# Constants in bf16, max-subtract matmuls behind other matmuls, and PSUM banks joined to the pool after the exponentials

## The chip, the cores and the metric

The kernel runs on one core of one Trainium2 chip. The metric is device microseconds of one execution; lower is better. A profile is one execution of its own: its span is about 2 us shorter than the time that the clock of the runs gives to the same execution (264.7 against 266.84 us for the profiled run of the kernel before).

## The reference

A block of two branches over one sequence of 2048 tokens of width 512, both fed by the same layernorm. Cut to what matters:

```python
xn = layernorm(x)
# branch A: 32 heads of 16, each token attends to 8 earlier tokens at distance 0, 2, ..., 14
q, k, v = split(xn @ wqkv)
logits  = sum_d q[s, d] * k[s - 2w, d] * scale          # w = 0..7, masked before the start
attn    = softmax(logits over w)
A       = (sum_w attn * v[s - 2w]) @ wo
# branch B: gated MLP with a mixing over tokens
z       = gelu(xn @ w_in);  z1, z2 = z[:, :896], z[:, 896:]
g       = w_sp @ layernorm(z2) + b_sp                    # w_sp is 2048 x 2048
B       = (z1 * g) @ w_out
out     = x + A + B
```

## The kernel before

The kernel is written as a list of operations with dependencies, estimated durations and priorities. A list scheduler runs once, when the kernel is built, and fixes the order of the instructions on each engine; the chip only sees that order and the semaphores. An operation's `margin` is added to the time at which the scheduler believes it to be ready. It is no wait on the chip: it makes the scheduler put other ready work of the same engine in front. PSUM is the buffer that matmuls write to, used here as eight banks of 128x512 f32; an eviction is the copy of a result out of its bank, after which the bank can be written again.

```python
# scheduler: when is an operation believed to be ready?
ready_t[u.seq] = max(d.done for d in u.deps) + self.HOP + u.margin

# constants: identity, head-sum matrix E and its transpose, loaded as f32 and cast on VectorE
_ldx(0, 1)
ld_cst = sc.dma(... e.dma_start(cfs, cdram.ap()) ...)        # 128 x 768 f32
_ldx(1, 1); _ldx(2, 1); _ldx(3, 1)                           # x tiles, then wq, wk, more x, wv, w_in
cv_id = sc.op("dve", ... tensor_copy(out=identb, in_=cf[:, 0:128]) ...)
# ... two more casts

banks = _Banks([0, 1, 2, 3])         # four PSUM banks rotate through T, QKV, Z2, Z1, G, output
# TensorE program: transposes of xn (T), then QKV (KQ), then V, Z2 (i = 0..15), Z1, G, output
# ... cut ...
# logits of row block u (512 tokens): VectorE multiplies q by the 8 shifted k (d1), TensorE sums
# over the 16 channels of a head with E (p1), four column groups t; u even uses banks 4,5, odd 6,7
d1 = sc.op("dve", ... tensor_tensor(out=pr, in0=qv, in1=kv, op=mult) ..., name="d1_%d_%d")
p1 = sc.op("pe", _p1, ..., prio=1, margin=pe_margin)         # pe_margin = 2500 ns
# after the fourth t: maximum over w, subtract it by a matmul, exponential, normalise
d2 = sc.op("dve", ... tensor_reduce(out=nm, in_=Lv, op=max, negate=True) ..., name="d2_%d")
p2 = sc.op("pe", _p2, [d2, cv_id], ..., name="p2_%d" % u, prio=1)      # no margin
ex = sc.op("act", ... activation(out=ep[:, u, :], in_=Lv, func=Exp, scale=0.25) ...)
# ... d3: sum, reciprocal, normalise on VectorE; later d4: probabilities times V on VectorE
```

In the text, "transpose" is T, "logit matmuls" are p1, "maximum" is d2 and "max-subtract matmuls" are p2. T, QKV, V, Z2 and Z1 are TensorE work with an eviction on ScalarE behind each group of four matmuls.

## Time and profile before

| | before |
|---|---|
| median of 15 runs | 267.33 us (266.36 to 268.94) |
| span of the profile | 264.7 us |
| TensorE (PE) busy | 94% |
| G stage starts in the chain of waits at | 127.04 us |
| last max-subtract matmuls at | 83.23 us |

The page's busy times and its 40 slices (each digit is the busy share of 6.6 us in tenths; PEclk is the clock that the record says was granted):

```profile
PE 247.8 (94%) x1655; PEld 118.5 (45%) x1682; DVE 196.8 (74%) x263; ACT 100.7 (38%) x166; POOL 55.5 (21%) x116
PE   6498996999996999999999999999999999999995
DVE  4798969999998999999322259799999997322332
PEclk9599999899999999999999999999999999999999
```

TensorE is full from the fourteenth slice on. VectorE (DVE) is full up to about the nineteenth, near 125 us. So there are two nearly full engines in the first 84 us; after that VectorE is still busy, but TensorE no longer waits for it.

The chain of waits of the kernel before, followed back from the last instruction (start, duration, what):

```profile
82.08 1.10 DVE negmax L665
...
83.23 0.60 PE ps L673 x2
83.83 19.04 PE ps L463 x100
...
127.04 8.20 PE ps L794 x38
```

Up to about 53 us the chain runs through QKV on TensorE and evictions on ScalarE, from there to 83 us mostly through VectorE; the last maximum (L665) releases the last max-subtract (L673), and from there on TensorE (L463 is Z2, L559 Z1, L794 G) follows itself without a gap. Whatever is won must be won before 84 us, and the kernel ends after the last max-subtract plus all the TensorE work that was not done before it.

The TensorE timeline of the kernel before (start, duration, engine, line, operation, tiles, count; in brackets the idle time in front and what ended it). L531 is QKV; 8 matmuls of 512 columns take 1.73 us start to start at full clock, 0.43 us each at half:

```profile
12.00 2.89 PE L531 MATMUL ps<-gh,rc 128*128 128x512 bf16 x7 [1.16 <-ACT gh L447]
14.95 1.89 PE L531 MATMUL ps<-gh,rc 128*128 128x512 bf16 x8
...
45.37 1.89 PE L531 MATMUL ps<-gh,rc 128*128 128x512 bf16 x4 [1.77 <-ACT gh L447]
47.48 2.22 PE L531 MATMUL ps<-gh,rc 128*128 128x512 bf16 x7 [0.22 <-issue]
...
79.54 1.69 PE L463 MATMUL ps<-gh 128*128 128x448 bf16 x8
83.23 0.60 PE L673 MATMUL ps<-negmax,identb 128*128 128x512 bf16 x2 [2.00 <-DVE negmax L665]
```

(The record of the first QKV matmul is missing here, as "x7" shows; the first weight load of the group is at 11.59 us. The 0.22 us in front of 47.48 us is such a missing record too, and no idle time.) Three losses stand out: a half-speed start, 1.77 us of waiting for a transpose eviction followed by about 3 us at half speed, and 2.00 us of waiting for the last maximum.

Why the 1.77 us: on ScalarE (ACT) that eviction (L447) stands behind the table load and the exponential of the first row block:

```profile
42.51 1.28 ACT L678 ACT_TABLE_LOAD   x1
43.80 1.02 ACT L678 ACTIVATE ep<-ps 128x1024 bf16<-128x1024 f32 x1
44.72 0.59 ACT L447 ACTIVATE gh<-ps 128x512 bf16<-128x512 bf16 x1
```

VectorE idles little in this stage. These are the largest idle times between 42 and 83 us, and the last maximum:

```profile
44.86 0.69 DVE L682 TENSOR_TENSOR gh<-ep 128x512 f32<-128x512 bf16 x1 [0.51 <-ACT ep L678]
53.57 1.22 DVE L665 TENSOR_REDUCE negmax<-ps 128x128 bf16<-128x1024 f32 x1 [0.71 <-PE ps L636]
81.45 0.51 DVE L490 TENSOR_SCALAR rb<-rb,mv,rs 128x896 bf16<-128x896 bf16 x1 [0.99 <-POOL rs L487]
82.00 1.17 DVE L665 TENSOR_REDUCE negmax<-ps 128x128 bf16<-128x1024 f32 x1
```

### The profile page before, as it was taken

To read this page: it belongs to the slowest core of one execution; us is meant where nothing else is said; L and a number is where in the kernel's file an instruction comes from. 1 tells how busy PE (TensorE), PEld (TensorE's weight loads), DVE (VectorE), ACT (ScalarE), POOL (GpSimd) and SP (SyncE) were. 2 spreads that over 40 slices of the span, in tenths; PEclk is the share of its full clock that TensorE was granted. 3 is DMA by queue.
4 is the path that set the end of the run, shared out by engine and by line. 5 is a ranking of instruction groups with operands and counts; after the bars stand their busy time and mean duration, and the time that the engine had idled before them with its cause. 6 is when DMAs were issued, how large, how long until landed. Compare 5 with 4: busy or idle time off the path is not lost.

```text
span 264.7 us, 4074 instructions
## 1 busy us (share of the span) xinstructions
PE 247.8 (94%) x1655; PEld 118.5 (45%) x1682; DVE 196.8 (74%) x263; ACT 100.7 (38%) x166; POOL 55.5 (21%) x116
## 2 busy tenths in 40 slices
PE   6498996999996999999999999999999999999995
PEld 5244453454453454444444444444444444444442
DVE  4798969999998999999322259799999997322332
ACT  3279876465577877677611111111011100000000
POOL 3568000201134544440000100000010030122200
PEclk9599999899999999999999999999999999999999
DMA  6999991030319920035699799788988860233331
GB/s 189 354 376 215 249 207 25 0 40 6 25 64 227 181 68 0 2 88 110 159 229 251 178 242 253 161 209 187 217 193 187 203 170 6 79 110 109 103 97 59
DMA packets 45969, 38.57 MB, mean 146 GB/s; under 512 B 34816, under 2 KB 42880, under 8 KB 43904
## 3 DMA queue, kind: packets, MB, share of 16 engines
q0 software_dynamic: 4160, 19.97, 34.0%
q1 hardware_dynamic: 41792, 18.35, 28.0%
q8 instruction: 13, 0.21, 0.4%
q14 instruction: 4, 0.03, 0.1%
HBM read 26.74 MB, written 3.15 MB: 113 GB/s over the span
## 4 chain that ended last, share of the span: by engine, by line
PE 77%; DVE 10%; ACT 6%; POOL 2%; issue 2%; DMA 1%; SPq 0%
PE ps L794 36%; PE ps L835 9%; PE ps L559 9%; PE ps L531 8%; PE ps L463 7%; DVE prod L629 6%; PE ps L846 5%; ACT kT L543 2%; ACT rc L512 2%; ACT gh L447 2%; DMA rc<-in_A_x_dram 1%; PE ps L636 1%; POOL pd_scratch L721 1%; ACT qT L543 1%; DVE negmax L665 1%
## 5 line engine op out<-in xcount | busy, mean ns | idle before, releaser
L531 PE MATMUL ps<-gh,rc 128*128 128x512 bf16 x180 | 46.1, 396 | 5.5 <-ACT gh L447 4.3
L794 PE MATMUL ps<-sa,rb 128*128 128x512 bf16 x220 | 48.3, 379 | 0.2
L794 PE MATMUL ps<-gh,rb 128*128 128x512 bf16 x219 | 48.2, 379 | 0.3
L787 ACT ACTIVATE ps<-xr 128x512 f32<-128x512 bf16 x28 | 16.8, 602 | 71.2 <-DVE rc L805 71.0
L629 DVE TENSOR_TENSOR prod<-qT,kT 128x4096 bf16<-128x4096 bf16 x16 | 36.2, 2276 | 2.5 <-ACT qT L543 1.4
L805 DVE TENSOR_TENSOR rc<-ps,rc 128x512 bf16<-128x512 f32 x28 | 19.2, 687 | 25.3 <-PE ps L794 25.3
L757 DVE TENSOR_TENSOR prod<-qT,vT 128x4096 bf16<-128x4096 bf16 x16 | 36.5, 2280 | 0.0
L794 PEld LDWEIGHTS ps<-gh,rb 128*128 128x128 bf16 x224 | 21.9, 98 | 26.4
L794 PEld LDWEIGHTS ps<-sa,rb 128*128 128x128 bf16 x224 | 21.9, 98 | 26.4
L856 DVE TENSOR_TENSOR stg<-ps,xr 128x512 bf16<-128x512 f32 x16 | 11.1, 692 | 26.9 <-PE ps L846 26.9
L729 POOL DMA_DIRECT2D qT<-pd_scratch x16 | 8.5, 530 | 104.1 <-DVE prod L757 44.4
L531 PEld LDWEIGHTS ps<-gh,rc 128*128 128x128 bf16 x192 | 18.1, 101 | 25.6 <-issue 4.8
L835 PE MATMUL ps<-sa,rc 128*128 128x512 bf16 x111 | 26.7, 379 | 0.1
L463 PE MATMUL ps<-gh 128*128 128x448 bf16 x128 | 25.0, 353 | 0.0
L559 PE MATMUL ps<-gh 128*128 128x512 bf16 x109 | 24.0, 379 | 0.2
L761 DVE TENSOR_TENSOR prod<-prod 128x2048 bf16<-128x2048 bf16 x16 | 19.5, 1219 | 0.1
L565 ACT ACTIVATE rc<-ps 128x512 bf16<-128x512 f32 x28 | 16.7, 595 | 6.7 <-PE ps L559 6.7
L470 ACT ACTIVATE rb<-ps 128x448 bf16<-128x448 f32 x32 | 16.8, 545 | 5.7 <-PE ps L463 5.6
L463 PEld LDWEIGHTS ps<-gh 128*128 128x128 bf16 x128 | 12.3, 98 | 11.8 <-ACT rb L470 0.4
L835 PEld LDWEIGHTS ps<-sa,rc 128*128 128x128 bf16 x112 | 11.0, 98 | 13.2
L559 PEld LDWEIGHTS ps<-gh 128*128 128x128 bf16 x112 | 11.0, 98 | 13.1
L846 PE MATMUL ps<-sa,kT 128*128 128x512 bf16 x62 | 16.2, 379 | 0.1
(55 smaller groups left out, 235.5 us busy)
## 6 DMA issues: line engine op xcount, KB each, us to landing
qT<-pd_scratch POOLq DMA_DIRECT2D x16, 1024.0 KB, 7.3
xr<-in_A_x_dram POOLq DMA_DIRECT2D x16, 128.0 KB, 2.4
out_dram<-stg SPq DMA_DIRECT2D x16, 128.0 KB, 1.7
gh<-in_B_w_in_dram SPq DMA_DIRECT2D x2, 896.0 KB, 10.1
rc<-in_A_wqkv_dram SPq DMA_DIRECT2D x2, 512.0 KB, 5.8
rc<-in_A_x_dram SPq DMA_DIRECT2D x2, 512.0 KB, 7.9
pd_scratch<-ep POOLq DMA_DIRECT2D x4, 256.0 KB, 10.1
sa<-in_B_w_out_dram SPq DMA_DIRECT2D x1, 896.0 KB, 9.1
```

Source lines behind the costliest of these rows:

```text
L463: ins = e.matmul(ps[:, bk, 0:448], xnT[:, k, 128 * i:128 * i + 128], w_in[:, k, 896 + 448 * hf:896 + 448 * hf + 448], start=(k == 0), stop ...
L470: ge = sc.op("act", lambda e, i=i, hf=hf, bk=bk: e.activation(out=z2[:, i, 448 * hf:448 * hf + 448], in_=ps[:, bk, 0:448], func=ACTF.Gelu_ ...
L531: ins = e.matmul(ps[:, bk, :], wP[:, k, which * 512 + 128 * t:which * 512 + 128 * t + 128], xnT[:, k, 512 * n:512 * n + 512], start=(k == ...
L559: ins = e.matmul(ps[:, bk, :], w_in[:, k, 128 * m:128 * m + 128], xnT[:, k, 512 * n:512 * n + 512], start=(k == 0), stop=(k == 3))
L629: d1 = sc.op("dve", lambda e, pr=pr, qv=qv, kv=kv: e.tensor_tensor(out=pr, in0=qv, in1=kv, op=ALU.mult), deps, dur=t_dve(4096, 2), name="d ...
L757: d4a = sc.op("dve", lambda e, b=b, vv=vv: e.tensor_tensor(out=tmp8.rearrange("p (w s) -> p w s", w=8), in0=pbS[b].rearrange("p (w s) -> p ...
L761: d4b = sc.op("dve", lambda e: e.tensor_tensor(out=tmpA, in0=tmp8[:, 0:2048], in1=tmp8[:, 2048:4096], op=ALU.add), [d4a, d4c_prev], dur=t_ ...
L787: pre = sc.op("act", lambda e, n=n, bk=bk: e.activation(out=ps[:, bk, :], in_=xrf[:, 512 * n:512 * n + 512], func=ACTF.Identity), [ld_bsp, ...
L794: ins = e.matmul(ps[:, bk, :], z2[:, k, 128 * m:128 * m + 128], slabs[n][:, k, :], start=False, stop=(k == 15), skip_group_check=True)
L805: uo = sc.op("dve", lambda e, n=n, m=m, bk=bk: e.tensor_tensor(out=z1T[:, m, 512 * n:512 * n + 512], in0=ps[:, bk, :], in1=z1T[:, m, 512 * ...
L835: ins = e.matmul(ps[:, bk, :], z1T[:, m, 128 * i:128 * i + 128], wout[:, m, :], start=(m == 0), stop=(m == 6 and not (with_attn and dbg_st ...
L846: ins = e.matmul(ps[:, bk, :], oT[:, t, 128 * i:128 * i + 128], wo_sb[:, t, :], start=False, stop=(t == 3))
```

## The change

The intent is to shorten the start (smaller constants, no casts, x first) and to let TensorE run ahead of the softmax: the max-subtract matmuls get the margin of the logit matmuls, and the banks of the logits join the pool of evictions once their exponential is done. Several load estimates are also retuned, which moves the order a little. The core of the diff:

```diff
-        ld_cst = sc.dma(lambda e: e.dma_start(cfs, cdram.ap()), "cst", 128 * 768 * 4, ...)
         _ldx(1, 1)
+        ld_cst = sc.dma(lambda e: e.dma_start(cst_sb[:, 0:ncst], cdb), "cst", 128 * ncst * 2, ...)  # ncst = 256
-        cv_id = sc.op("dve", ... tensor_copy(out=identb, in_=cf[:, 0:128]) ...)     # and two more casts
+        cv_id = ld_cst
...
-        wraw = sa[:, 8192:8192 + 2048]...    # wv loaded here, permuted into wP
+        wvP = sa[:, 8192:8192 + 2048]...     # wv loaded into wP ahead of x tiles 12-15, permuted to here
...
-                p2 = sc.op("pe", _p2, [d2, cv_id], ..., name="p2_%d" % u, prio=1)
+                p2 = sc.op("pe", _p2, [d2, cv_id], ..., name="p2_%d" % u, prio=1, margin=pe_margin)
...
+            banks.add(4, exp_ops[2])          # usable after the third exponential
+            banks.add(5, exp_ops[2])
+            for i in range(NT):               # moved here from in front of the softmax
+                make_Z2(i, 0)
+                make_Z2(i, 1)
+            banks.add(6, exp_ops[3])          # usable after the fourth
+            banks.add(7, exp_ops[3])
...
-                              "sl1", ..., deps=lst, ...          # second transposing load of w_sp: after the permutations
+                              "sl1", ..., deps=[last_v_mm], ...  # after the last V matmul
```

The compiled order on TensorE changes in two places that matter. The last transpose now comes before the first max-subtract (it came after: at 42.65 us, behind the max-subtract at 42.21 us). The last max-subtract stands behind 20 Z2 matmuls after the last logit matmuls (it stood behind 8).

More of the change, by code (lines that the diff above doesn't have):

```diff
@@ L52, in op, with dma @@
         return o
-    def dma(self, fn, chan, nbytes, deps=(), rate=300.0, name="", prio=5, lat=2000.0,
+    def dma(self, fn, chan, nbytes, deps=(), rate=330.0, name="", prio=5, lat=1600.0,
             issue=650.0, serial=True, eng="sp"):
@@ L217, in __init__, with add @@
         self.banks = list(banks)
+        self.i = 0
         self.g = 0
-        self.evac = {}
+        self.last = {}
+        self.first = {}
+        self.bank_of = {}
+    def add(self, bank, first_dep):
+        if bank not in self.banks:
+            self.banks.append(bank)
+            self.first[bank] = first_dep
     def next(self):
@@ L223, in next @@
         self.g += 1
-        b = self.banks[g % len(self.banks)]
-        war = self.evac.get(g - len(self.banks))
+        b = self.banks[self.i % len(self.banks)]
+        self.i += 1
+        war = self.last.get(b, self.first.get(b))
+        self.bank_of[g] = b
         return g, b, war
     def set_evac(self, g, op):
-        self.evac[g] = op
+        self.last[self.bank_of[g]] = op
 def build_kernel(nc, A_x, A_wqkv, A_wo, B_x, B_w_in, B_w_sp, B_b_sp, B_w_out, out,
@@ L256, in build_kernel @@
                  gh[:, 8192:16384].rearrange("p (k t) -> p k t", k=16)]
-        wraw = sa[:, 8192:8192 + 2048].rearrange("p (k f) -> p k f", k=4)
+        wvP = sa[:, 8192:8192 + 2048].rearrange("p (k f) -> p k f", k=4)
         wout = sa[:, 0:3584].rearrange("p (m d) -> p m d", m=7)
@@ L263, in build_kernel @@
         z1T = rc[:, :].rearrange("p (m s) -> p m s", m=7)
-        identb = sb("identb", [128, 128], BF16)
-        Eb = sb("Eb", [128, 128], BF16)
+        cst_sb = sb("cst_sb", [128, 768 if (with_attn and pb_mode == "pe") else 256], BF16)
+        identb = cst_sb[:, 0:128]
+        Eb = cst_sb[:, 128:256]
         ones = sb("ones", [128, 128], BF16)
@@ L283, in build_kernel @@
         s4 = gh[:, 15360:16384].bitcast(F32)
-        cfs = None
         ps = es.enter_context(nc.psum_tensor("ps", [128, 8, 512], F32))
@@ L290, in build_kernel @@
             prod = sb("prod", [128, 2, 4096], BF16)
-            cfs = prod[:, 0, 0:1536].bitcast(F32)
             negmax = sb("negmax", [128, 2, 128], BF16)
@@ L294, in build_kernel @@
             pd = nc.dram_tensor("pd_scratch", (4, 4, 8, 8, 4, 128), BF16, kind="Internal")
-            ETn = sb("ETn", [128, 4, 128], BF16)
+            ETn = cst_sb[:, 256:768].rearrange("p (t m) -> p t m", t=4) if pb_mode == "pe" else None
             s2 = sb("s2", [128, 256], F32)
@@ L303, in build_kernel @@
             tmpB = prod[:, 1, 2048:3072]
-        if cfs is None:
-            cfs_t = sb("cfs", [128, 768], F32)
-            cfs = cfs_t[:, :]
-        cf = cfs[:, 0:256]
         sems = {e: sem("s_" + e) for e in ("pe", "act", "dve", "pool")}
@@ L313, in build_kernel @@
         chan_sems = {c: sem("c_" + c) for c in chan_names}
-        cnp = np.zeros((128, 768), np.float32)
-        cnp[:, 0:128] = np.eye(128, dtype=np.float32)
+        ncst = 768 if (with_attn and pb_mode == "pe") else 256
+        cnp = np.zeros((128, ncst), np.uint16)
+        ONE = 0x3F80
         for p in range(128):
+            cnp[p, p] = ONE
             for t in range(4):
-                cnp[p, 128 + 32 * t + 8 * t + (p // 16)] = 1.0
+                cnp[p, 128 + 32 * t + 8 * t + (p // 16)] = ONE
                 h = p % 32
-                if h // 8 == t:
+                if ncst > 256 and h // 8 == t:
                     for d in range(16):
-                        cnp[p, 256 + 128 * t + 8 * d + (h % 8)] = 1.0
+                        cnp[p, 256 + 128 * t + 8 * d + (h % 8)] = ONE
         cdram = nc.inline_tensor(cnp, "cblob")
+        cdb = cdram.ap().bitcast(BF16)
         sc = _Sched()
@@ L334, in _ldx @@
             o = sc.dma(lambda e, src=src: e.dma_start(xs[:, i0:i0 + n, :], src), "x%d" % i0, n * 128 * 512 * 2,
-                       name="ld_x%d" % i0, prio=prio, eng=eng, issue=500.0 + 500.0 * n)
+                       name="ld_x%d" % i0, prio=prio, eng=eng, issue=150.0 + 500.0 * n)
             for i in range(i0, i0 + n):
@@ L338, in build_kernel @@
         _ldx(0, 1)
-        ld_cst = sc.dma(lambda e: e.dma_start(cfs, cdram.ap()), "cst", 128 * 768 * 4, name="ld_cst", prio=0,
+        _ldx(1, 1)
+        ld_cst = sc.dma(lambda e: e.dma_start(cst_sb[:, 0:ncst], cdb), "cst", 128 * ncst * 2, name="ld_cst", prio=0,
                         issue=600.0)
-        _ldx(1, 1)
         _ldx(2, 1)
         _ldx(3, 1)
-        ld_wv = None
+        ld_wq = ld_wk = ld_wv = None
         if with_attn:
             ld_wq = sc.dma(lambda e: e.dma_start(wP[:, :, 0:512], wq3[:, :, 0:512]), "wq",
-                           512 * 512 * 2, name="ld_wq", prio=0, issue=1100.0)
+                           512 * 512 * 2, name="ld_wq", prio=0, issue=700.0)
             ld_wk = sc.dma(lambda e: e.dma_start(wP[:, :, 512:1024], wq3[:, :, 512:1024]), "wk",
-                           512 * 512 * 2, name="ld_wk", prio=0, issue=1100.0)
+                           512 * 512 * 2, name="ld_wk", prio=0, issue=700.0)
         _ldx(4, 2)
@@ L352, in build_kernel @@
         _ldx(8, 4)
+        if with_attn:
+            ld_wv = sc.dma(lambda e: e.dma_start(wP[:, :, 1024:1536], wq3[:, :, 1024:1536]), "wv",
+                           512 * 512 * 2, name="ld_wv", prio=1, issue=700.0)
         _ldx(12, 4)
-        if with_attn:
-            ld_wv = sc.dma(lambda e: e.dma_start(wraw[:, :, :], wq3[:, :, 1024:1536]), "wv",
-                           512 * 512 * 2, name="ld_wv", prio=1, issue=1100.0)
         src2 = B_w_in[:, 896:1792].rearrange("(k p) f -> p k f", p=128)
@@ L370, in build_kernel @@
                          [ms_nh], dur=1400, name="act_warm", prio=1)
-        cv_id = sc.op("dve", lambda e: e.tensor_copy(out=identb[:, :], in_=cf[:, 0:128]), [ld_cst],
-                      dur=200, name="cv_id", prio=0)
-        cv_E = sc.op("dve", lambda e: e.tensor_copy(out=Eb[:, :], in_=cf[:, 128:256]), [ld_cst],
-                     dur=200, name="cv_E", prio=1)
-        cv_ET = None
-        if with_attn:
-            cv_ET = sc.op("dve", lambda e: e.tensor_copy(out=ETn[:, :, :].rearrange("p t m -> p (t m)"),
-                                                         in_=cfs[:, 256:768]), [ld_cst], dur=300, name="cv_ET", prio=2)
+        cv_id = ld_cst
+        cv_E = ld_cst
+        cv_ET = ld_cst
         E3 = Eb[:, :].rearrange("p (t m) -> p t m", t=4)
@@ L505, in build_kernel @@
             for k in range(4):
-                src0 = wraw[:, k, :]
+                src0 = wP[:, k, 1024:1536]
                 pitch = src0.ap[0][0]
                 src = _ap(src0, src0.offset, [[pitch, 128], [128, 4], [1, 16], [16, 8]])
-                dst0 = wP[:, k, 1024:1536]
+                dst0 = wvP[:, k, :]
                 dpitch = dst0.ap[0][0]
@@ L517, in build_kernel @@
             perm[2] = lst
-            ld_sl[1] = sc.dma(lambda e: e.dma_start_transpose(slabs[1], B_w_sp[512:1024, :]),
-                              "sl1", 512 * 2048 * 2, deps=lst, rate=280.0, name="ld_sl1",
-                              prio=2, issue=7600.0)
         else:
@@ L523, in build_kernel, with make_KQ, _kq @@
                               "sl1", 512 * 2048 * 2, rate=280.0, name="ld_sl1", prio=2, issue=7600.0)
-        def make_KQ(n, which, t):
+        def make_KQ(n, which, t, c0=0, nc_=512):
             g, bk, war = banks.next()
-            def _kq(e, n=n, which=which, t=t, bk=bk):
+            s0 = 512 * n + c0
+            def _kq(e, which=which, t=t, bk=bk, s0=s0, nc_=nc_):
                 ins = None
                 for k in range(4):
-                    ins = e.matmul(ps[:, bk, :], wP[:, k, which * 512 + 128 * t:which * 512 + 128 * t + 128],
-                                   xnT[:, k, 512 * n:512 * n + 512], start=(k == 0), stop=(k == 3))
-                return ins
-            mm = sc.op("pe", _kq, perm[which] + [war, st["pe_prev"]] + xnT_ev[4 * n:4 * n + 4],
-                       dur=4 * t_pe(512), name="kqmm%d_%d_%d" % (n, which, t))
+                    wsl = wvP[:, k, 128 * t:128 * t + 128] if which == 2 else \
+                        wP[:, k, which * 512 + 128 * t:which * 512 + 128 * t + 128]
+                    ins = e.matmul(ps[:, bk, 0:nc_], wsl, xnT[:, k, s0:s0 + nc_], start=(k == 0), stop=(k == 3))
+                return ins
+            mm = sc.op("pe", _kq, perm[which] + [war, st["pe_prev"]] + xnT_ev[s0 // 128:(s0 + nc_) // 128],
+                       dur=4 * t_pe(nc_), name="kqmm%d_%d_%d_%d" % (n, which, t, c0))
@@ L536, in make_KQ @@
             st["pe_prev"] = mm
             if which == 1:
-                dst = kT[:, t, 16 + 512 * n:16 + 512 * n + 512]
+                dst = kT[:, t, 16 + s0:16 + s0 + nc_]
             elif which == 0:
-                dst = qT[:, t, 512 * n:512 * n + 512]
+                dst = qT[:, t, s0:s0 + nc_]
             else:
-                dst = vT[:, t, 16 + 512 * n:16 + 512 * n + 512]
-            ev = sc.op("act", lambda e, dst=dst, bk=bk: e.activation(out=dst, in_=ps[:, bk, :], func=ACTF.Identity),
-                       [mm], dur=t_act(512), name="kqev%d_%d_%d" % (n, which, t), prio=3)
+                dst = vT[:, t, 16 + s0:16 + s0 + nc_]
@@ L545, in make_KQ @@
+            ev = sc.op("act", lambda e, dst=dst, bk=bk, nc_=nc_: e.activation(out=dst, in_=ps[:, bk, 0:nc_],
+                                                                             func=ACTF.Identity),
+                       [mm], dur=t_act(nc_), name="kqev%d_%d_%d_%d" % (n, which, t, c0), prio=3)
             banks.set_evac(g, ev)
             if which == 2:
-                v_ev[(n, t)] = ev
+                v_ev.setdefault((n, t), []).append(ev)
             else:
-                kq_ev[(n, which, t)] = ev
+                kq_ev.setdefault((n, which, t), []).append(ev)
@@ L569, in make_Z1 @@
             z1_ev[(n, m)] = ge
+        last_v_mm = None
         if with_attn:
@@ L585, in build_kernel @@
             last_v_mm = st["pe_prev"]
-            for i in range(NT):
-                make_Z2(i, 0)
-                make_Z2(i, 1)
-        else:
-            make_T(0)
-            for i in range(NT):
-                if i + 1 < NT:
-                    make_T(i + 1)
-                make_Z2(i, 0)
-                make_Z2(i, 1)
-        alias_deps = [tr_ops[NT - 1]] + ([last_v_mm] if with_attn else [])
-        for n in range(4):
-            for m in range(7):
-                make_Z1(n, m, alias_deps)
-        last_z1_mm = st["pe_prev"]
-        pe_prev = st["pe_prev"]
+            ld_sl[1] = sc.dma(lambda e: e.dma_start_transpose(slabs[1], B_w_sp[512:1024, :]),
+                              "sl1", 512 * 2048 * 2, deps=[last_v_mm], rate=280.0, name="ld_sl1",
+                              prio=2, issue=7600.0)
         d4_done = {}
@@ L623, in build_kernel @@
                 pr = prod[:, pb_i, :].rearrange("p (w s) -> p w s", w=8)
-                deps = [kq_ev[(u, 0, t)], kq_ev[(u, 1, t)], ms_halo, cv_id, cv_E, cv_ET]
+                deps = kq_ev[(u, 0, t)] + kq_ev[(u, 1, t)] + [ms_halo, cv_id, cv_E, cv_ET]
                 if u > 0:
-                    deps.append(kq_ev[(u - 1, 1, t)])
+                    deps += kq_ev[(u - 1, 1, t)]
                 if idx >= 2:
@@ L675, in _p2 @@
                     return ins
-                p2 = sc.op("pe", _p2, [d2, cv_id], dur=2 * t_pe(512), name="p2_%d" % u, prio=1)
+                p2 = sc.op("pe", _p2, [d2, cv_id], dur=2 * t_pe(512), name="p2_%d" % u, prio=1, margin=pe_margin)
                 p2_ops[u] = p2
@@ L695, in build_kernel @@
                 d3n_ops[u] = d3n
+        if with_attn:
+            banks.add(4, exp_ops[2])
[3 more added lines that the diff above has]
+                make_Z2(i, 1)
+            if pb_mode == "dma":
+                banks.add(6, exp_ops[3])
+                banks.add(7, exp_ops[3])
+        else:
+            make_T(0)
+            for i in range(NT):
+                if i + 1 < NT:
+                    make_T(i + 1)
+                make_Z2(i, 0)
+                make_Z2(i, 1)
+        alias_deps = [tr_ops[NT - 1]] + ([last_v_mm] if with_attn else [])
+        for n in range(4):
+            for m in range(7):
+                make_Z1(n, m, alias_deps)
+        last_z1_mm = st["pe_prev"]
+        pe_prev = st["pe_prev"]
+        if with_attn:
             if dbg_stage < 2:
@@ L753, in build_kernel @@
                 vv = _ap(v0, v0.offset, [[pitch_v, 128], [-2, 8], [1, 512]])
-                deps = evs + [v_ev[(u, t)], ms_halo, last_p1, d4b_prev]
+                deps = evs + v_ev[(u, t)] + [ms_halo, last_p1, d4b_prev]
                 if u > 0:
-                    deps.append(v_ev[(u - 1, t)])
+                    deps += v_ev[(u - 1, t)]
                 d4a = sc.op("dve", lambda e, b=b, vv=vv: e.tensor_tensor(
```

## The prediction

> **What bounds the kernel now.** TensorE. The page gives PE 94% busy and 77% of the chain that ended last. From 84 us on it never waits: the chain shows matmuls back to back (49 of 128x512 in 10.74 us, 219 ns each) to 261.7 us. So all that can be won lies before 84 us. There the timeline of PE shows:
> - First QKV matmul at 12.00 us, behind x loads, casts and layernorm.
> - 12.0 to 14.5 us: matmuls at 0.43 us instead of 0.216, about 1.25 us lost.
> - 21 to 32 us: about 1.5 us waiting for ScalarE, 100% busy from 20 to 30 us (four permutations of 1.14 us).
> - 43.6 us: 1.77 us waiting for the transpose eviction queued on ScalarE behind the table load (1.28 us) and exponential (1.02 us), then half-speed matmuls to 48.9 us: about 1.8 us more.
> - Max-subtract matmuls (L673) waiting for VectorE's maximum: 0.35, 0.50 and, at 81.2, 2.00 us.
> But VectorE is nearly full too: in its timeline it idles under 3 us from 42.1 to 83.2 us. It is the second limit of this stage.
>
> **What the change does.**
> - Constants as bf16, 64 KB instead of 384 KB, behind the second x tile; three casts (0.23, 0.22, 0.41 us) leave VectorE's startup. QKV start 12.0 to about 10.4 us.
> - The slow-clock interval at the start stays. The Trainium skill ("TensorE: Matmul & The Clock Gate", Part 1) says full clock comes only after a busy window of about 3.4 us; the 3.5 us of half-speed matmuls after 45.4 us agree. An earlier start may run half-speed longer: I count 1.2 of 1.6 us.
> - Instruction order: the last transpose and its eviction now come before the first exponential, so the 1.77 us wait and the half speed after it should vanish.
> - The last max-subtract now stands behind 20 Z2 matmuls instead of 8 (12 x 0.19 = 2.3 us), filling the 2.00 us wait; two more PSUM banks after the third exponential let PE run ahead.
> - V permutation: same four copies. Second w_sp transpose moves from 29 us to about 72 us, needed only near 147 us. No effect expected.
>
> **How much counts.** TensorE alone would save about 7 us, but its logit matmuls wait for VectorE's products (2.28 us each), whose work is unchanged. VectorE gets only the earlier start (1.2 us) and about 1 us of its idle back, so its last maximum moves from 83.2 to about 81 us. At that point TensorE has 12 more Z2 matmuls done. Gain: 2.1 + 2.3 = about 4.3 us. The rest reappears as 1 to 2 us waits of logit matmuls (L636) around 48 and 63 us.
>
> **Prediction: 263.4 us, 80% range 261.5 to 265.6.** Faster by over 2%: 0.27; within 2%: 0.71; slower: 0.02.
>
> **Signs.** Right: first QKV matmul near 10.4 us; no wait for the eviction near 43 us; last max-subtract near 81 us with at most 1 us wait; new L636 waits for VectorE; unchanged matmul pitch after 84 us; G stage starting near 122.7 instead of 127.0 us. Wrong: start unchanged; VectorE's last maximum still near 83 us; a new low-clock slice.
>
> **What would make it wrong.** New waits of about 2 us trigger half speed (loses 1 to 2 us); the deferred transpose load crowds the probability loads at 75 to 90 us and delays the layernorm of Z2; or VectorE recovers more idle than I think (gain up to 7 us).

## The result and the profile after

| | before | after |
|---|---|---|
| median | 267.33 us (15 runs) | 262.81 us (12 runs, 262.01 to 263.45) |
| ratio | | 0.9819, 95% interval 0.9798 to 0.9841 |
| span of the profile | 264.7 us | 260.8 us |
| last maximum (VectorE) starts | 82.00 us | 80.45 us |
| last max-subtract (TensorE) starts | 83.23 us | 81.68 us |
| Z2 matmuls still to do behind it | 100 | 88 |
| G stage starts in the chain | 127.04 us | 123.10 us |

Ratios are the mean time of one kernel's fast runs over that of the kernel before in the same rounds, so they are not quite the ratio of the medians. The interval includes 0.98, so it is open whether the gain is above 2%. The outputs of all ten experiments are on record as correct.

The page's busy times and slices after, and the chain:

```profile
PE 246.7 (95%) x1654; PEld 118.3 (45%) x1682; DVE 196.1 (75%) x260; ACT 98.9 (38%) x166; POOL 56.5 (22%) x116
PE   6697999897999999999999999999999999999995
PEclk9589999999999999999999999999999999999999
```

```profile
80.53 1.10 DVE negmax L656
...
81.68 0.60 PE ps L664 x2
82.28 16.65 PE ps L466 x88
...
123.10 8.20 PE ps L809 x38
```

The chain has the same shape, and the whole gain of this pair of profiles can be read off it: the last max-subtract starts 1.55 us earlier, and the Z2 work behind it takes 16.65 instead of 19.04 us because 12 of its matmuls were done before. That is 3.94 us, and the G stage starts 3.94 us earlier. Behind it nothing changed: the runs of 49 matmuls take 10.74 us in both chains. The timed runs give more than this pair, 0.0181 times 267.5 us = 4.8 us; the profiled run of the kernel before (266.84 us) was faster than its median.

The TensorE timeline after (L534 is QKV, L627 the logit matmuls, L664 the max-subtract, L466 Z2):

```profile
10.54 3.19 PE L534 MATMUL ps<-gh,rc 128*128 128x512 bf16 x7 [1.16 <-ACT gh L450]
13.96 2.20 PE L534 MATMUL ps<-gh,rc 128*128 128x512 bf16 x8
...
21.80 1.90 PE L534 MATMUL ps<-gh,rc 128*128 128x512 bf16 x7 [1.51 <-ACT gh L450]
...
42.85 2.76 PE L534 MATMUL ps<-gh,rc 128*128 128x512 bf16 x11
...
50.95 0.63 PE L627 MATMUL ps<-prod,cst_sb 128*32 128x128 bf16 x32 [0.54 <-DVE prod L620]
...
65.46 0.63 PE L627 MATMUL ps<-prod,cst_sb 128*32 128x128 bf16 x32 [1.73 <-DVE prod L620]
...
77.41 3.96 PE L466 MATMUL ps<-gh 128*128 128x448 bf16 x20
81.68 0.60 PE L664 MATMUL ps<-negmax,cst_sb 128*128 128x512 bf16 x2 [0.31 <-DVE negmax L656]
```

The 1.77 us wait is gone, the 2.00 us wait has become 0.31 us, and two new waits for VectorE's products appear (0.54 and 1.73 us). The VectorE timeline after, at the first and the last maximum:

```profile
40.75 1.22 DVE L656 TENSOR_REDUCE negmax<-ps 128x128 bf16<-128x1024 f32 x1
...
79.90 0.51 DVE L493 TENSOR_SCALAR rb<-rb,mv,rs 128x896 bf16<-128x896 bf16 x1 [0.99 <-POOL rs L490]
80.45 1.17 DVE L656 TENSOR_REDUCE negmax<-ps 128x128 bf16<-128x1024 f32 x1
```

One thing does not fit: QKV starts about 1.5 us earlier, but the first maximum, at 40.75 us, is only 0.18 us earlier than before (40.93 us). Did the bf16 constants win nothing? The experiments had to say.

### The profile page after: what moved, and what is told of

It reads as the page before. It is cut to its first block, busy times and chain, and to the rows that moved or that the text cites. A ratio compares the mean times of both kernels' runs of the same rounds, so it can differ in the third digit from the quotient of the medians.

```text
span 260.8 us, 4072 instructions
## 1 busy us (share of the span) xinstructions
PE 246.7 (95%) x1654; PEld 118.3 (45%) x1682; DVE 196.1 (75%) x260; ACT 98.9 (38%) x166; POOL 56.5 (22%) x116
## 4 chain that ended last, share of the span: by engine, by line
PE 75%; DVE 14%; ACT 3%; POOL 3%; issue 3%; DMA 1%
PE ps L809 37%; PE ps L850 9%; PE ps L562 9%; DVE prod L620 8%; PE ps L534 7%; PE ps L466 6%; PE ps L861 5%; DVE negmax L656 1%; DVE rinv L679 1%; ACT kT L545 1%; ACT gh L450 1%; POOL rs L426 1%; PE ps L445 1%; DVE ep L682 1%; DMA rc<-in_A_x_dram 1%
## 5 line engine op out<-in xcount | busy, mean ns | idle before, releaser
L772 DVE TENSOR_TENSOR prod<-qT,vT 128x4096 bf16<-128x4096 bf16 x16 | 36.6, 2286 | 11.2 <-DMA qT<-pd_scratch 11.1
L534 PE MATMUL ps<-gh,rc 128*128 128x512 bf16 x119 | 31.0, 397 | 3.7 <-ACT gh L450 3.1
L871 DVE TENSOR_TENSOR stg<-ps,xr 128x512 bf16<-128x512 f32 x16 | 11.1, 691 | 23.8 <-PE ps L861 23.8
L466 PE MATMUL ps<-gh 128*128 128x448 bf16 x128 | 24.9, 353 | 0.0
L534 PEld LDWEIGHTS ps<-gh,rc 128*128 128x128 bf16 x128 | 11.9, 101 | 16.4 <-issue 3.1
L466 PEld LDWEIGHTS ps<-gh 128*128 128x128 bf16 x128 | 12.4, 98 | 11.6
L736 POOL DMA_DIRECT2D pd_scratch<-ep x4 | 8.4, 2112 | 39.9 <-DVE ep L682 35.6
```

The source lines that it names most:

```text
L466: ins = e.matmul(ps[:, bk, 0:448], xnT[:, k, 128 * i:128 * i + 128], w_in[:, k, 896 + 448 * hf:896 + 448 * hf + 448], start=(k == 0), stop ...
L534: ins = e.matmul(ps[:, bk, 0:nc_], wsl, xnT[:, k, s0:s0 + nc_], start=(k == 0), stop=(k == 3))
L772: d4a = sc.op("dve", lambda e, b=b, vv=vv: e.tensor_tensor(out=tmp8.rearrange("p (w s) -> p w s", w=8), in0=pbS[b].rearrange("p (w s) -> p ...
```

## The experiments

Three theories were set against each other. The order theory says that the gain is the new TensorE order, that is, the one line with the margin. The startup theory says that a good part is the bf16 constants and the earlier x. The bank theory says that it is the larger pool of banks.

Gains below are differences of ratios. The experiments were timed in other rounds than the changed kernel, on several chips, each beside runs of the kernel before; a difference of two ratios is uncertain by about 0.7 to 1.1 us (an estimate: the half-widths of the two 95% intervals, added in quadrature).

### b_margin: the margin alone, on the kernel before

```diff
-                p2 = sc.op("pe", _p2, [d2, cv_id], dur=2 * t_pe(512), name="p2_%d" % u, prio=1)
+                p2 = sc.op("pe", _p2, [d2, cv_id], dur=2 * t_pe(512), name="p2_%d" % u, prio=1, margin=pe_margin)
```

> The kernel before with one line of the change only: the estimate of when the max-subtract matmuls become ready is raised by 2.5 us, so the TensorE order is the changed kernel's from 40 us on (last transpose before the first exponential, 20 instead of 8 Z2 matmuls before the last max-subtract). Constants in f32, four banks, old load order. Order theory: this is nearly the whole gain, 263.3 to 264.2 us, no wait for the eviction near 43 us. Startup theory (bf16 constants and x first give 1.5 us of the gain): 265 us or more. Bank theory (more PSUM banks give the gain): at most 1 us faster than before.

Measured: 265.2 us (264.43 to 265.51, 6 runs), ratio 0.9906 (0.9882 to 0.9931). The order theory's number was missed: the margin alone wins about 2.5 us, not 3.3 to 4.2, and the time falls in the range of the startup theory (265 us or more). The eviction wait near 43 us is gone, the last max-subtract waits 0.30 us, and a new wait of 0.89 us for an eviction stands in front of the Z2 matmuls at 87.12 us, behind the last exponential. (Its line is shown with a_4banks, where it is the same.)

### a_nomargin: the changed kernel without the margin

The same line is put back in the changed kernel; everything else stays.

> The changed kernel without that one line; bf16 constants, load order, Z2 creation order and extra banks stay. Order theory: 266.5 to 267.3 us, nearly all of the gain lost, and the 1.8 us wait near 43 us and the 2 us wait near 81 us are back. Startup theory: about 265.8 us, 1.5 us of the gain stay. Bank theory: about 263 us.

Measured: 266.25 us (264.78 to 267.69, 6 runs), ratio 0.9948 (0.9915 to 0.9981). This lies between the order and the startup theory: 3.5 us of the changed kernel's gain are lost (0.9948 less 0.9819, times 267.5 us), but about 1.4 us stay. Both waits are back:

```profile
44.08 2.76 PE L534 MATMUL ps<-gh,rc 128*128 128x512 bf16 x12 [1.77 <-ACT gh L450]
...
81.10 0.61 PE L664 MATMUL ps<-negmax,cst_sb 128*128 128x512 bf16 x2 [2.00 <-DVE negmax L656]
```

The same 1.77 us wait is followed here by 12 matmuls in 2.76 us, which is full speed. In the kernel before's profile the matmuls behind it ran at half speed. So the half speed after that wait is not a constant part of the loss. (The profiled run is the fastest of the six; how often the half speed came is taken up in the explanation below.)

### a_4banks: the changed kernel on four banks

```diff
-            banks.add(4, exp_ops[2])
-            banks.add(5, exp_ops[2])
             for i in range(NT):
                 make_Z2(i, 0)
                 make_Z2(i, 1)
-                banks.add(6, exp_ops[3])
-                banks.add(7, exp_ops[3])
```

> The changed kernel with the two additions of banks left out: Z2, Z1, G and output stay on four PSUM banks; same TensorE order. Order theory: within 0.5 us of the changed kernel (262.8), since TensorE did not wait for a bank after 84 us before either; at most a 0.4 us wait behind the last exponential. Bank theory: 264.5 us or more.

Measured: 264.01 us (263.33 to 264.48, 6 runs), ratio 0.9862 (0.9838 to 0.9886), about 1.15 us slower than the changed kernel (0.9862 less 0.9819, times 267.5 us). I had expected at most 0.5 us; the bank theory's 264.5 us or more was not reached either. The wait is the same as in b_margin, and ScalarE shows why (timelines of TensorE and ScalarE of this run):

```profile
86.50 13.79 PE L466 MATMUL ps<-gh 128*128 128x448 bf16 x72 [0.89 <-ACT rb L473]
```

```profile
82.27 1.28 ACT L669 ACT_TABLE_LOAD   x1
83.56 1.02 ACT L669 ACTIVATE ep<-ps 128x1024 bf16<-128x1024 f32 x1
84.60 1.28 ACT L473 ACT_TABLE_LOAD   x1
85.90 2.87 ACT L473 ACTIVATE rb<-ps 128x448 bf16<-128x448 f32 x6
```

The last exponential with its two table loads keeps ScalarE from evicting Z2 for 3.6 us. TensorE fills four banks in 4 x 4 x 0.19 = 3.0 us and then stands still. With the banks 4 and 5 it has 4.5 us of room and the wait is gone. The Trainium skill, "Perfetto Trace Analysis", Optimization Strategy, says of "consistent bubbles" that they can mean too few buffers; this trace shows the same cause in a single bubble of 0.89 us, which no average shows. The same wait did not cost anything in the order before, because TensorE's own 2.00 us wait came first: in the kernel before ScalarE loads the table of the exponential at 81.83 us, during that wait, and evicts again at 86.20 us, 2.5 us after Z2 goes on at 83.67 us and so within the 3.0 us of four banks. The timed runs agree: the additional banks are in a_nomargin as well, and it is no faster than b_const below, which has none of them.

### a_permlate: the V permutations later

The reading was that the four permutation copies on ScalarE (1.14 us each, at 17 to 27 us) eat the earlier start, because the 1.51 us wait at 20.3 us is for an eviction behind them.

```diff
+            for k in range(4):
+                lst[k].deps.append(xnT_ev[12 + k])
             for n in range(4):
                 for t in range(4):
                     make_KQ(n, 2, t)
```

> The changed kernel with the four permutations of the V weights on ScalarE spread to one each after the evictions of transposes 12 to 15 (about 30 to 42 us) instead of 17 to 27 us. Theory: the 1.46 us of earlier QKV start are lost because the permutations stand in front of the transpose evictions; without them the 1.5 us wait at 20.3 us and the 0.39 us wait at 31 us vanish, the first max-reduce moves from 40.8 to about 39.2 us, and the run is 1.0 to 1.9 us faster than the changed kernel (about 261.3 us). Rival: the layernorm on VectorE or loads of x set the pace there, then no change (262.8 us).

Measured: 262.68 us (262.45 to 263.12, 5 runs), ratio 0.9817 (0.9794 to 0.9841): no change that can be told apart from 0.9819. In its profile the wait shrinks from 1.51 to 0.95 us only, and the wait at 31 us stays at 0.40 us. Most of it seems to be the plain latency of an eviction whose transpose stands directly in front of the first matmul that needs it; this run does not show that by itself, but in a_all below, with the transposes earlier, both waits are gone. My theory was mostly wrong; at most about 0.6 us hang on the permutations, and the runs do not resolve that.

### b_const and a_f32const: the constants alone, and all but the constants

b_const makes only the constants' part of the change on the kernel before. a_f32const takes only that part back in the changed kernel:

```diff
-        _ldx(1, 1)
-        ld_cst = sc.dma(lambda e: e.dma_start(cst_sb[:, 0:ncst], cdb), "cst", 128 * ncst * 2, ...)
+        ld_cst = sc.dma(lambda e: e.dma_start(cfs, cdram.ap()), "cst", 128 * 768 * 4, ...)
+        _ldx(1, 1)
-        cv_id = ld_cst
+        cv_id = sc.op("dve", lambda e: e.tensor_copy(out=identb, in_=cfs[:, 0:128]), [ld_cst], ...)   # and two more
```

> The kernel before with only the constants changed: bf16 load of 64 KB behind the second x tile, no casts. After the first four runs the gain looks like a sum of three parts: order about 2.3 us, banks about 1.2, startup about 1.2. If the parts add, this run is 1.2 us faster than before (about 266.3 us), with the QKV start at 10.0 to 10.6 us instead of 12.0 and most of the 1.5 us still there at the first max-reduce when the slow clock ends early, less when it ends late. Rival (the earlier start is always eaten by the slow clock and by ScalarE before 42 us): within 0.4 us of before.

> The changed kernel with only the constants put back (f32 load of 384 KB ahead of the second x tile, three casts on VectorE). If the parts add: about 1.2 us slower than the changed kernel (264.0 us), TensorE order and banks unchanged. Rival (startup gain eaten): within 0.4 us of 262.8 us.

Measured: b_const 266.38 us (265.37 to 267.57, 6 runs), ratio 0.9941 (0.9914 to 0.9968); a_f32const 264.98 us (264.07 to 265.32, 6 runs), ratio 0.9881 (0.9857 to 0.9904). The constants are worth 1.6 us on the kernel before and 1.7 us on the changed one (0.9881 less 0.9819, times 267.5 us). Within the noise the parts add, and the rival that the earlier start is always eaten is refuted.

Then why did the pair of profiles show only 0.18 us? Because the slow clock at the start does not end at a fixed time. Here is the same place in a_f32const, where the second group of 8 is still slow (2.77 against 1.89 us), and the window from 13 to 15 us of that run. Its columns are the window, its length, busy time and count of instructions of PE, PEld, DVE, ACT and POOL, then granted clock, DMA share and GB/s:

```profile
11.93 3.19 PE L537 MATMUL ps<-gh,rc 128*128 128x512 bf16 x7 [1.16 <-ACT gh L453]
...
15.35 2.77 PE L537 MATMUL ps<-gh,rc 128*128 128x512 bf16 x8
```

```profile
13.00:15.00 2.00, 2.00 (x6) 0.69 (x5) 1.93 (x7) 0.60 (x1) 1.37 (x4) 1.00 1.10 352
```

In the profile of the kernel before the matmuls are at full speed from the second group on; in that of the changed kernel half speed reaches into the second group; in a_f32const it fills most of it, and the first maximum is at 42.71 us. The reading that fits all of this is that the one profile of the kernel before was lucky at the start, and a lucky start was compared with an ordinary one. The clock events in the traces support it: the slow stretch ends at 14.45 us in the kernel before, but at 16.02 and 17.11 us in the other two profiles with f32 constants (b_margin, a_f32const); in the six profiles with bf16 constants and without a_warm's matmuls it ends between 12.44 and 15.36 us, in the changed kernel's at 14.58 us. The clock column above reads 1.00 while the matmuls are 0.43 us apart because that trace holds no clock event before 17.11 us, and the view counts such time as full clock. So at the start look at the spacing of the matmuls.

The profile of b_const, taken from its slowest run, shows a second thing. Its span of 265.4 us is longer than that of the kernel before, because behind its 2.00 us wait for the last maximum TensorE runs at half speed for 3.4 us, and the 100 Z2 matmuls take 20.76 instead of 19.04 us:

```profile
82.75 20.76 PE L451 MATMUL ps<-gh 128*128 128x448 bf16 x100
```

By their granted clocks (0.981 or less), such a second slow stretch came in 9 of the 11 runs of the kernel before in these rounds and in 2 of the 6 of b_const. So a part of b_const's 1.6 us may be that and not the start. The 1.7 us from a_f32const have less of this rival: its order has neither the 1.77 nor the 2.00 us wait, and one of its six runs reads 0.981.

### a_warm: TensorE kept busy at the start

```diff
-                 with_attn=True, warm=40, ...
+                 with_attn=True, warm=48, ...
+            nfill = {1: 18, 2: 4, 3: 18}.get(i, 0)       # behind the transposes of tiles 1, 2, 3
+            if nfill:
+                # nfill dummy matmuls 128x128 of ones into bank 7, unused this early
+                st["pe_prev"] = sc.op("pe", _fill, [tr], dur=nfill * 56.0, name="fill%d" % i, prio=5)
```

> The changed kernel with 8 more dummy matmuls at the start and 18, 4 and 18 dummy matmuls (128x128, into the unused bank 7) behind the second, third and fourth transpose, where TensorE waits about 1 us each. If the slow clock from 8 to 14.4 us comes from TensorE idling between 5 and 10.5 us, the matmuls from 10.5 us on run at 0.216 us, about 2 us are won at 15 us, and 0.5 to 2 us remain at the end (about 261.5 us). Rival: VectorE's layernorm (two tiles in 2.1 us) sets the pace behind it, or the clock does not follow: no change, 262.8 us.

Measured: 262.08 us (261.91 to 263.01, 5 runs), ratio 0.9783 (0.976 to 0.9806), about 1 us better than the changed kernel. QKV runs at full speed from its first matmul:

```profile
10.12 1.67 PE L542 MATMUL ps<-gh,rc 128*128 128x512 bf16 x7
13.06 0.40 PE L445 MATMUL ps<-cst_sb,rc 128*128 128x128 bf16 x4 [1.26 <-DVE rc L429]
13.30 1.89 PE L542 MATMUL ps<-gh,rc 128*128 128x512 bf16 x8
```

About 1.3 us of what the clock gives are lost again at once, because the next transpose now waits for VectorE's layernorm. The first maximum moves from 40.75 to 39.78 us, and the span shrinks by the same amount, from 260.8 to 259.8 us. So filling TensorE's idle time takes the slow stretch at the start away, and in this pair of profiles the time won there reaches the end in full. The clock records of all five timed runs read 1.000, but so do three of a_f32const's six, whose profile starts slow; the spacing of the matmuls is the evidence.

### a_margin: fill the new waits for VectorE

```diff
-  p1: margin=pe_margin
+  p1: margin=pe_margin + {(2, 0): 1000.0, (3, 0): 1000.0}.get((u, t), 0.0)
-  p2: margin=pe_margin
+  p2: margin=pe_margin + (800.0 if u == 3 else 0.0)
```

> The changed kernel with the logit matmuls of the third and fourth row block set 4 matmuls (0.86 us) later in the TensorE order, and the last max-subtract 4 Z2 matmuls later. The changed kernel waits there 0.54, 1.73 and 0.31 us for VectorE. If those waits are plain gaps that other matmuls can fill, 0.54 + 0.86 + 0.31 = 1.7 us are won (261.1 us). Rival (VectorE sets the pace up to the last maximum, so a gap filled here opens elsewhere): within 0.5 us of 262.8 us.

Measured: 262.45 us (261.44 to 262.8, 5 runs), ratio 0.9785 (0.9761 to 0.981). By the ratio that is 0.9 us better than the changed kernel, about half of the 1.7 us that I expected, and hardly clear of the noise (the intervals overlap, and the medians are 0.36 us apart). The profile shows a gain of 0.8 us and why it is no more:

```profile
65.42 0.63 PE L627 MATMUL ps<-prod,cst_sb 128*32 128x128 bf16 x32 [0.87 <-DVE prod L620]
...
76.52 4.71 PE L466 MATMUL ps<-gh 128*128 128x448 bf16 x24
81.65 0.60 PE L665 MATMUL ps<-negmax,cst_sb 128*128 128x512 bf16 x2 [0.42 <-DVE negmax L657]
```

The last maximum did not move (80.42 against 80.45 us); the wait in front of the 65 us logit matmuls was halved, but another opened at the second max-subtract (0.41 us). What counts is one thing only: 24 instead of 20 Z2 matmuls are done before the last max-subtract, 4 x 0.19 = 0.8 us, and the span is 260.0 instead of 260.8 us. VectorE fixes when the last maximum is there; TensorE gains only by what it has done by then.

### a_all2 and a_all: the edits together

a_all2 is a_warm, a_margin and a_permlate together, with Z2 starting on bank 0 instead of bank 4. a_all also places each transpose one QKV group earlier, and gives the maxima the highest priority in the scheduler, which the expectation does not mention.

```diff
+            banks.i = 0                       # both
-                        if n < 3 and gi % 2 == 0:          # a_all only
-                            make_T(4 * (n + 1) + gi // 2 - 1)
+                        if n < 3 and gi % 2 == 1:
+                            make_T(4 * (n + 1) + gi // 2)
-  d2: prio=2                                              # a_all only
+  d2: prio=0
```

> Three edits of the earlier runs together on the changed kernel: dummy matmuls that keep the clock up (0.97 us in its trace), later logit and max-subtract matmuls (0.8 us), V permutations spread to 30 to 42 us (0.6 us), and Z2 starting on bank 0 instead of bank 4. If VectorE is paced by its start and TensorE by (time of VectorE's last maximum, minus the Z2 matmuls done before it), the three act at different places and add: 2.3 us under the changed kernel, about 260.5 us, last maximum near 79 us. Rival (one limit behind all three): no better than the best single edit, 261.8 us or more.

> As a_all2, and the transposes of the next column block are placed one QKV group earlier, so that the first matmul that needs the last transpose's eviction no longer stands right behind it (waits of 1.51 and 0.39 us in the changed kernel). If those waits are a matter of placement only: another 0.8 to 1.3 us, 259.2 to 259.7 us, and the first max-reduce near 38 us. If the layernorm on VectorE cannot feed the earlier transposes, the waits move to the transposes and nothing is won over a_all2 (260.5 us); if the order that the schedule then chooses runs into the third exponential, it is slower.

Measured: a_all2 260.88 us (260.38 to 261.65, 5 runs), ratio 0.9759 (0.9742 to 0.9777), about 1.6 us better than the changed kernel (2.3 us were expected) and the best of the study. a_all 262.43 us (262.35 to 264.38, 5 runs), ratio 0.9827 (0.98 to 0.9855), no better than the changed kernel. In a_all2 the last maximum is at 78.39 us and the span is 258.1 us. In a_all the early waits of 1.51 and 0.39 us are gone, as hoped, but the scheduler then chose another order: the last maximum is sent behind four more layernorm statistics on VectorE, and TensorE waits for it again (whether the earlier transposes or the priority made it choose so was not separated):

```profile
81.77 1.21 DVE L667 TENSOR_REDUCE negmax<-ps 128x128 bf16<-128x1024 f32 x1
```

```profile
83.03 0.60 PE L675 MATMUL ps<-negmax,cst_sb 128*128 128x512 bf16 x2 [2.41 <-DVE negmax L667]
```

Behind this 2.41 us wait TensorE runs at half speed again, from 83.85 to 87.26 us by the clock events (Z2 matmuls 0.37 instead of 0.19 us apart), about 1.7 us lost on the chain. All five timed runs read a clock of 0.987 to 0.993, those of a_all2 0.999 or more.

## Why the prediction was right, point by point

Predicted were 263.4 us (261.5 to 265.6); measured were 262.81 us. The forecast of the ratio is 263.4 / 267.69 = 0.984, the measured one 0.9819.

| part | predicted | measured, by what |
|---|---|---|
| earlier start (constants) | 1.2 us | 1.6 us alone (b_const), 1.7 us in the changed kernel (a_f32const) |
| order, with the banks | 3.1 us (4.3 less 1.2) | 3.5 us (a_nomargin against the changed kernel) |
| of which the banks | not sized apart | 1.15 us in the new order (a_4banks), none in the old (a_nomargin against b_const) |
| moved w_sp load, permutations | none | none that shows: in the old order everything but the margin (a_nomargin, 0.9948) wins no more than the constants alone (b_const, 0.9941) |

- *TensorE bounds the kernel after 84 us, and all gains lie before.* Right. The chain behind the last max-subtract is the same but for the 12 Z2 matmuls.
- *QKV start from 12.0 to about 10.4 us.* Right within 0.2 us: 10.54 us in the profile by the same record. *Of 1.6 us I count 1.2.* The deduction for a longer slow clock was a guess about one profile. The Trainium skill, "TensorE: Matmul & The Clock Gate", Part 1, says that the window is free-running, so that the number of slow matmuls varies from run to run. The profiles agree: the second QKV group takes 1.89 us in the kernel before, 2.20 us after and 2.77 us in a_f32const. In the mean of the runs no such loss shows: 1.6 and 1.7 us, with the reserve made at b_const.
- *The 1.77 us wait and the half speed after it should vanish.* Both vanished. The half speed is no fixed loss of 1.8 us: behind the same wait a_nomargin runs at full speed. But it is frequent. The profile of the kernel before has two slow stretches by its clock events (7.62 to 14.45 and 45.17 to 48.58 us), a granted clock of 0.981 together; 23 of the 31 runs of the kernel before that stand beside the experiments read 0.979 to 0.981, 3 of the 12 of a_nomargin and b_const, and none of the 12 of the changed kernel (0.986 or more). So part of the gain seems to be that both long waits are gone which such a stretch can follow; how large a part, the runs do not separate. In the forecast it entered only through VectorE (below).
- *TensorE would save 7 us, but VectorE lets only 4.3 through; the rest reappears as waits of the logit matmuls.* Right, and the useful step of the prediction. The new waits are 0.54 us at 50 us and 1.73 us at 64 us (predicted: 1 to 2 us around 48 and 63 us), and the last max-subtract starts at 81.68 us (predicted: near 81) with 0.31 us of wait. a_margin confirms it from the other side: with the last maximum in place, the gain is the number of Z2 matmuls done before it.
- *VectorE gets the earlier start (1.2 us) and about 1 us of its idle back.* About 0.6 us too much for this pair (2.2 us predicted, 1.55 us measured), and wrong in its division: the first maximum came 0.18 us earlier and the last 1.55 us, so in this pair 1.37 us were idle time and 0.18 us the start. The 1.37 us split again: from the first to the last maximum it takes 41.07 us in the kernel before, 40.23 and 40.24 us in b_const and a_nomargin (the old order, at full speed there), and 39.70 us in the changed kernel. So 0.83 us were the half speed of that one profile and 0.54 us the order. The timed runs give the start 1.6 us.
- *Two more banks let PE run ahead.* Said, but not sized. It was worth 1.15 us, and without the banks the new order alone wins only 2.5 us, less than the 3.1 us forecast for it. That the total came out so near is in part luck: the wait for a bank that the new order would have caused was not foreseen, and the banks that the change added took it away.
- *Deferred transpose load crowds the probability loads and delays the layernorm of Z2.* The crowding came, the harm did not. The moved load is issued from 72.50 us on, over 14.28 us (before: at 29.04 us, 9.66 us), and in the products with V VectorE now waits 11.1 us for the probability loads, where it waited 0.0 us before:

```profile
L772 DVE TENSOR_TENSOR prod<-qT,vT 128x4096 bf16<-128x4096 bf16 x16 | 36.6, 2286 | 11.2 <-DMA qT<-pd_scratch 11.1
```

  The three profiles with the early load have 0.0 to 0.3 us of this wait, the nine with the late one 7.7 to 14.8 us. It costs nothing here, because from 83 us on the chain holds nothing but TensorE until the output is written. The layernorm of Z2 was not delayed up to the last maximum: VectorE's wait for GpSimd in front of it is 0.99 us in both profiles.

## What to carry to other kernels

When two engines are nearly full in one stage, take the gain from the engine that releases the last joint step: the other wins only the work it has finished by then, so put independent work in front of the step that waits. More buffers can be worthless in one order and worth a microsecond in another, so test them in the order that will ship. Time won in front of a stage with an unsteady clock is not to be read from one pair of profiles; timed runs of each part settle it.

## What the Trainium skill lacked or had wrong

- "TensorE: Matmul & The Clock Gate", Why this matters for your kernels: it asks for no TensorE idle gaps over about 3 us. Shorter ones can do it, but do not always: in the profile of the kernel before half speed follows a wait of 1.77 us (4 matmuls in 1.89 us at 45.37 us), in b_const one of 2.00 us and in a_all one of 2.41 us; in a_nomargin and b_const the same 1.77 us wait is followed by full speed. An estimate from the traces, which no run tested: the clock events lie 3.41 us apart or multiples of it, and on this grid TensorE's idle time within one interval sorts the cases. 1.93 us (kernel before, 41.75 to 45.17 us), 2.00 us (b_const, 80.22 to 83.63 us) and 2.41 us (a_all, 80.44 to 83.85 us) were followed by half speed; 1.77 us (b_const, 42.67 to 46.08 us) and 1.73 us (changed kernel, 62.36 to 65.78 us) were not, and in a_nomargin the wait falls on two intervals (1.21 and 0.92 us).
- The same page names dummy matmuls as a warm-up only for benchmarks, and says in Part 4 that transposes do not engage the full clock; no run here tests that. It does not draw the advice for a kernel in which transposes that wait for VectorE stand between a warm-up and the first matmuls. Here 48 instead of 40 dummy matmuls at the start and 40 more between the transposes won about 1 us (a_warm, 0.9783 against 0.9819).
- "ScalarE: Activation LUTs", What ACT_TABLE_LOAD costs: it gives about 2.66 us in all for a switch of table set, 1.28 us of load and 1.38 us of drain. Here the load takes 1.28 us, and the exponential starts 0.01 us after it ends (42.51 + 1.28 against 43.80 us); the drain does not show there. Nor does it show in front of the load: in a_4banks the load at 82.27 us starts 0.02 us after the activation before it ends (81.71 + 0.54 us).
